# Where a block's token sums and low parts are made, GpSimd or VectorE, in a fused attention and two-layer network kernel

## The chip, the cores and the metric

The kernel runs on one core of a Trainium2 chip. The metric is the device time of one execution in microseconds. Before the change three runs took 752.82, 753.55 and 754.12 us, a median of 753.55.

## The reference, cut to what matters

Attention over 4 x 576 tokens with 8 heads of 64 gives x of 2304 tokens x 512. A first network layer follows, and a second one, which is the stage that the change touches. All is f32.

```
x = maximum(maximum(x @ w1, x @ w2), x @ w3) @ w_out        # 512 -> 768 -> 512
h = x @ w_in                                                # 512 -> 2048
g = maximum(h, 0) + alpha * minimum(h, 0)
out = g @ w_out2                                            # 2048 -> 512
```

## The kernel before, in words

f32 products are made of fp32r parts: a factor is split into a high part (a cast to fp32r) and a low part (the rest, by a subtraction), and three products (high-high, high-low, low-high) are added up in PSUM.

**The second layer** takes 2304 tokens in 3 blocks of 768 (`blk`), and 2048 hidden rows as 8 pairs of 128 rows (`q`), so there are 24 steps, n = 8 blk + q; n is counted from 0 and `NQ` is 8. Both matrix products are done by a scheme of seven products in place of eight for a 2x2 block split (`PRODUCTS`). It needs sums of quarter blocks of x: of the rows b11, b12, b21, b22 that `load_x2` fetches (four DMAs of 192 KB, 128x384 each, in this order) `sum_x2` makes four subtractions, the first of them t3 = b22 - b12, and seven tiles come of it; two halves (`half` 0 and 1) of the 512 columns are done so. `split_x2` makes high and low part of each tile. For blocks 1 and 2 the fourteen tiles go to DRAM (`xd`, L857) and come back through `fetch_x2` (L863) while the last pair of the block before is computed.

**Inside one n**, `h_products` (L1162) makes seven products, each of six matmuls of 384 columns into one PSUM bank (L1176). Two banks (tag `ph`) take turns, so a product needs the bank of the one two before it, and VectorE's addition (L1182) or ScalarE's copy (L1186) empties it. The activation (L1124 to L1128), the sums for the second matrix product (L1160) and its splits (L976 high on ScalarE, L977 low on VectorE) are queued between the products by `defer` and `due`. Behind each product the main loop (L1239) also advances `o_units`, the second matrix product of the n before, by one or two units of three matmuls of 256 columns (L983).

**At a block's end** (q = 7) `o_units` has 84 units instead of 12: the "kept" products k = 0, 1, 2 over all eight pairs (`kept_units`), whose g parts `prepare` splits a few units ahead, and the output additions (`quarter`, L1001 to L1035) with the stores (L1006). `ended` runs 48 of them ahead of the first product of n = 8, 16 and (after the last n) at the end; the other 36 follow behind the products of n = 8, five behind each. A wide kept step is a matmul of 512 columns (L989) and one of 256 (L993); a narrow one has three of 256 columns (L983). With a wide step the bank holds two halves, and each output quarter takes two additions.

**Queues.** Every engine runs its instructions in the order of the code. SyncE issues all DMAs in that order too: the weights of the first product (`load_h`, L871), of the second (`load_ow`, L883, one behind every sixth unit), output stores, and the stores and loads of the tiles. The tiles of the third block's preparation come from small pools: two row pairs (`xsp`), three sums (`tsp`) and two tiles for high and low part (`xst`).

**The third block's preparation before** goes by the table `early`: at the first product of n = 1 and n = 9 the four loads are issued; one subtraction on GpSimd (L828) stands behind each product from the fourth on; in n = 2 to 7 and 10 to 14 the first product is followed by one or two splits (L208 high on ScalarE, L211 low on GpSimd), and behind the fourth product `early_store` issues their stores. The same helpers prepare the second block earlier, in the first layer's last part, on GpSimd too.

Of the kernel before, what the change touches and what calls it, by code (L numbers as in the profile page):

```python
# [10 lines left out]
F32 = mybir.dt.float32  # L11
F32R = mybir.dt.float32r
U32 = mybir.dt.uint32
AF = mybir.ActivationFunctionType
ALU = mybir.AluOpType
# [6 lines left out]
P = 128  # L22
# [10 lines left out]
HB = BLK // 2  # L33
NBLK = NT // BLK
NQ = NF2 // 2
# [125 lines left out]
def attention_maxout_prelu_kernel(  # L161
# [13 lines left out]
    nc = tc.nc  # L175
# [41 lines left out]
    def pool(stack, name, bufs, side="left"):  # L217
        return stack.enter_context(tc.tile_pool(name=name, bufs=bufs, side=side, reuse_waits="tile"))
# [5 lines left out]
    xd = [None] + [[[dram.tile([P, 2, HB], F32, name=f"xd{blk}_{k}_{i}") for i in range(2)]  # L224
                    for k in range(7)] for blk in range(1, NBLK)]
# [455 lines left out]
    def last_net(b):  # L681
# [121 lines left out]
        for hf in range(2):  # L803
            for dc in range(NCC):
# [5 lines left out]
    PRODUCTS = (((0, 0), "11"), ((2, 256), "T2"), ((0, 256), "21"), ((2, 0), "T3"),  # L810
                ((1, 0), "T1"), ((1, 256), "T4"), ((3, 0), "22"))
    xs, x2h = {}, {}

    def load_x2(blk, i, pool, tag):

        rows = [pool.tile([P, 2, HB], F32, tag=tag, name=tag) for _ in range(2)]
        for r, t in enumerate(rows):
            for h in range(2):
                nc.sync.dma_start(t[:, h, :], x2d[2 * blk + h][:, i + 2 * r, :])
        return rows  # L820

    def sum_x2(blk, i, rows, engine, later=None):

        b11, b12, b21, b22 = (t[:, h] for t in rows for h in range(2))
        t2, t3, t4 = (tsp.tile([P, HB], F32, tag="t", name="t") for _ in range(3))
        for out_, x, y in ((t3, b22, b12), (b12, b12, b11), (t2, b22, b12), (t4, b21, t2)):
            def one(out_=out_, x=x, y=y):
                engine.tensor_tensor(out=out_, in0=x, in1=y, op=ALU.subtract)  # L828

            if later is None:  # L830
                one()
            else:
                later.append(one)
        for name, x in (("11", b11), ("T1", b12), ("21", b21), ("22", b22), ("T2", t2),
                        ("T3", t3), ("T4", t4)):
            xs[blk, name, i] = x

    def split_x2(blk, k, i, pool, tag, lo_engine=nc.vector):

        t = pool.tile([P, 2, HB], F32R, tag=tag, name=tag)  # L840
        split(t[:, 0], t[:, 1], xs.pop((blk, PRODUCTS[k][1], i)), nc.scalar, lo_engine)
        return t

    early_rows, early_parts = {}, []

    def early_load(blk, i, pool, tag):
        early_rows[blk, i] = load_x2(blk, i, pool, tag)

    def early_sums(blk, i, later=None):
        sum_x2(blk, i, early_rows.pop((blk, i)), nc.gpsimd, later)  # L850

    def early_split(blk, i, k, pool=None):
        early_parts.append((blk, k, i, split_x2(blk, k, i, pool or xst, "xst", nc.gpsimd)))

    def early_store():
        for blk, k, i, t in early_parts:
            nc.sync.dma_start(xd[blk][k][i], t.bitcast(F32))  # L857
        early_parts.clear()
# [19 lines left out]
    def load_ow():  # L878
        key = next(ow_next, None)
        if key is not None:  # L880
            _, which, a, i = key
            t = words[key] = wp.tile([P, 2, DM], F32R, tag="w", name="w")
            nc.sync.dma_start(t.bitcast(F32), (od1 if which == "o1" else od2)[a][i])  # L883
# [4 lines left out]
    for b in range(B):  # L888
        first, last = (-32, -8) if b == 0 else ((b - 1) * NUNITS + (16 if b == 1 else 3), b * NUNITS - 3)
        step = (last - first) / (len(ATT_UNITS) + 2)  # L890
# [22 lines left out]
    xsp = pool(ctx, "xsp", 2, "right")  # L913
    tsp = pool(ctx, "tsp", 3, "right")
    xst = pool(ctx, "xst", 2, "right")
# [64 lines left out]
    def o_products(g, w, off, t, bank, half, first, last):  # L980

        for i, (gi, wi) in enumerate(PAIRS):
            nc.tensor.matmul(bank[:, NH * half:NH * (half + 1)], g[:, gi, t * P:(t + 1) * P],  # L983
                             w[:, wi, off:off + NH], start=first and i == 0, stop=last and i == 2)
# [54 lines left out]
    def o_units(n):  # L1039
        blk, q = divmod(n, NQ)  # L1040
        if q == NQ - 1:

            first = [ps_h.tile([P, DM], F32, tag="ph", name="ph") for _ in range(2)]
            for p in range(2):
                yield from kept_units(blk, 0, p, first, parts_.pop((blk, 0, p)))
        for k in range(4):
            w = words[blk, "o1", q, k // 2]
            for t in range(3):
                s = 3 * k + t
                if q == 0 and s % 2 == 0:  # L1050
                    accs[s // 2] = ps_o.tile([P, DM], F32, tag="po", name="po")
                o_products(gts[n, k], w, NH * (k % 2), t, accs[s // 2], s % 2,
                           q == 0 and s % 2 == 0, q == NQ - 1 and s % 2 == 1)
                if q == NQ - 1 and s % 2 == 1:
                    for z in (s - 1, s):
                        drains.append((blk, *divmod(z, 3), accs[s // 2], z % 2))
                if k % 2 == 1 and t == 2:
                    load_ow()
                yield
            if q == NQ - 1 and k > 0:  # L1060
                prepare(blk)
        if q < NQ - 1:
            return
        for k in range(3):
            wide = [None, [0, 1, 2], [0, 1] if blk == NBLK - 1 else [0, 1, 2]][k]
            banks = [ps_o.tile([P, DM], F32, tag="po", name="po") for _ in range(3)] if k else first
            for p in range(0 if k else 2, NQ):
                for _ in range(1 if k == 0 or p == 0 else 2):
                    if len(parts_) < AHEAD:
                        prepare(blk)  # L1070
                yield from kept_units(blk, k, p, banks, parts_.pop((blk, k, p)), wide)
# [3 lines left out]
    def kept_units(blk, k, p, banks, g, wide=None):  # L1075
        w = words[blk, "o2", k, p // 2]
        for t in range(3):
            if wide is None:
                o_products(g, w, NH * (p % 2), t, banks[t // 2], t % 2,
                           p == 0 and t % 2 == 0, p == NQ - 1 and t > 0)  # L1080
            elif t in wide:
                wide_products(g, w, NH * (p % 2), t, banks[t], p == 0, p == NQ - 1)
            else:
                o_products(g, w, NH * (p % 2), t, banks[t], 0, p == 0, p == NQ - 1)
            if p == NQ - 1 and wide is not None:
                drains.append((blk, 4 + k, t, banks[t], None if t in wide else 0))
            elif p == NQ - 1 and t > 0:
                for z in ((0, 1) if t == 1 else (2,)):
                    drains.append((blk, 4 + k, z, banks[z // 2], z % 2))
            if p % 2 == 1 and t == 2:  # L1090
                load_ow()
            last = k == 2 and p == NQ - 1
            if t == 2 or last:
                for _ in drains[:] if last else drains[:2]:
                    quarter(*drains.pop(0))
            yield
# [131 lines left out]
    def ended(outs):  # L1228
        for i in range(48):
            if i in (0, 2, 4, 6, 8):  # L1230
# [1 line left out]
                due(i == 8)  # L1232
            next(outs, None)

    early = {1: [(0, None)], 2: [(0, 0)], 3: [(0, 1)], 4: [(0, 2)], 5: [(0, 3), (0, 4)], 6: [(0, 5)], 7: [(0, 6)],
             9: [(1, None)], 10: [(1, 0)], 11: [(1, 1), (1, 2)], 12: [(1, 3)], 13: [(1, 4), (1, 5)], 14: [(1, 6)]}
    sums_left = []
    outs = iter(())
    for n in range(NQ * NBLK):  # L1239
        blk, q = divmod(n, NQ)  # L1240
        units_before = [i * 12 // 7 for i in range(8)]
        if blk and q == 0:
            ended(outs)
            units_before = [5 * i + (i == 7) for i in range(8)]
        for i, _ in enumerate(h_products(n)):
            if q == NQ - 1 and blk + 1 < NBLK:
                fetch_x2(blk + 1, i)
            if i == 0:
                for half, k in early.get(n, ()):
                    if k is None:  # L1250
                        early_load(2, half, xsp, "xs")
                        early_sums(2, half, sums_left)
                    else:
                        early_split(2, half, k)
            if i == 3:
                early_store()
            if i > 2 and sums_left:
                sums_left.pop(0)()
            for _ in range(units_before[i + 1] - units_before[i]):
                next(outs, None)  # L1260
        assert next(outs, None) is None
        outs = o_units(n)
# [55 lines left out]
```

## Time and profile before

| what | before |
|---|---|
| median of 3 runs | 753.55 us (752.82 to 754.12) |
| the profiled execution's own time | 751.83 us |
| its span, first to last instruction | 750.0 us |
| TensorE (PE) busy | 733.9 us, 98% |
| VectorE (DVE) busy | 641.4 us, 86% |
| ScalarE (ACT) busy | 461.8 us, 62% |
| GpSimd (POOL) busy | 53.1 us, 7% |
| granted TensorE clock, mean | 1.000 |

PE is the matmuls, PEld the weight loads beside them, SPq the DMA issues of SyncE. Times in rows are microseconds from the span's start, the duration of one instruction is in microseconds or, in lists of one line's instructions, in ns. The bracket at a row's end is the idle time of the engine before it and what ended it. The end of a matmul is modelled, so the pace of TensorE is read from start to start. The second layer begins at 387.7 us.

### The profile page before, as it was taken

To read this page: it belongs to the slowest core of one execution; us is meant where nothing else is said; L and a number is where in the kernel's file an instruction comes from. 1 tells how busy PE (TensorE), PEld (TensorE's weight loads), DVE (VectorE), ACT (ScalarE), POOL (GpSimd) and SP (SyncE) were. 2 spreads that over 40 slices of the span, in tenths; PEclk is the share of its full clock that TensorE was granted. 3 is DMA by queue.
4 is the path that set the end of the run, shared out by engine and by line. 5 is a ranking of instruction groups with operands and counts; after the bars stand their busy time and mean duration, and the time that the engine had idled before them with its cause. 6 is when DMAs were issued, how large, how long until landed. Compare 5 with 4: busy or idle time off the path is not lost.

```text
span 750.0 us, 15973 instructions
## 1 busy us (share of the span) xinstructions
PE 733.9 (98%) x5544; PEld 709.6 (95%) x5544; DVE 641.4 (86%) x1689; ACT 461.8 (62%) x1249; POOL 53.1 (7%) x64
## 2 busy tenths in 40 slices
PE   5899999999999999999999999999999999999997
PEld 4699999999999999999999999999999999999996
DVE  5899999898899899658779888888988888988897
ACT  6987889568675787332255666624665654556571
POOL 1000000000000000024504010000401000000000
PEclk9999999999999999999999999999999999999999
DMA  7576769896999865679899889999888999767362
GB/s 250 168 228 225 244 204 344 330 343 222 326 337 335 303 225 192 225 288 325 296 324 378 270 281 317 393 387 356 308 306 292 368 402 354 283 232 258 118 200 67
DMA packets 88928, 211.95 MB, mean 283 GB/s; under 512 B 11024, under 2 KB 41232, under 8 KB 88848
## 3 DMA queue, kind: packets, MB, share of 16 engines
q1 hardware_dynamic: 88848, 210.94, 80.0%
q8 instruction: 44, 0.72, 0.4%
q14 instruction: 36, 0.29, 0.1%
HBM read 154.80 MB, written 56.10 MB: 281 GB/s over the span
## 4 chain that ended last, share of the span: by engine, by line
PE 81%; DVE 7%; DMA 5%; ACT 4%; issue 2%; SPq 0%; DVEq 0%; ACTq 0%
PE ph L1176 21%; PE bank L577 19%; PE po L983 13%; PE bank L599 9%; PE bank L750 4%; PE ph L983 3%; PE po L989 3%; DMA wh<-w 3%; PE bank L314 2%; PE bank L389 2%; ACT e L329 2%; PE bank L364 2%; PE po L993 2%; DMA raw<-in_w 1%; DVE g L977 1%
## 5 line engine op out<-in xcount | busy, mean ns | idle before, releaser
L1176 PE MATMUL ph<-x,w 128*128 128x384 f32 x990 | 200.5, 337 | 1.0 <-DVE c L1182 1.0
L577 PE MATMUL bank<-x,w 128*128 128x288 f32 x1440 | 197.9, 296 | 0.2
L577 PEld LDWEIGHTS bank<-x,w 128*128 128x128 f32 x1440 | 191.9, 188 | 2.5 <-DVE w L256 0.6
L1176 PEld LDWEIGHTS ph<-x,w 128*128 128x128 f32 x990 | 166.3, 188 | 2.5 <-DVE c L1182 1.4
L983 PE MATMUL po<-w,g 128*128 128x256 f32 x888 | 130.9, 281 | 0.0
L983 PEld LDWEIGHTS po<-w,g 128*128 128x128 f32 x888 | 125.3, 189 | 0.7
L1182 DVE TENSOR_TENSOR c<-ph,c 128x384 f32<-128x384 f32 x165 | 89.1, 552 | 29.4 <-PE ph L1176 25.7
L976 ACT CAST g<-c 128x384 fp32r<-128x384 f32 x93 | 47.0, 505 | 97.0 <-DVE c L1160 53.9
L599 PE MATMUL bank<-h,w 128*128 128x288 f32 x576 | 79.3, 297 | 0.3 <-DVE nm L322 0.3
L599 PEld LDWEIGHTS bank<-h,w 128*128 128x128 f32 x576 | 76.9, 188 | 1.2 <-DVE nm L322 0.5
L253 ACT CAST w<-word 128x512 fp32r<-128x512 f32 x100 | 57.7, 590 | 26.6 <-DMA wh<-w 10.2
L329 ACT ACTIVATE e<-e,nm 96x128 f32<-96x128 f32 (+2 forms) x176 | 68.5, 403 | 8.4 <-DVE nm L322 8.4
L256 DVE TENSOR_TENSOR w<-word,w 128x512 fp32r<-128x512 f32 x100 | 62.9, 640 | 9.0 <-ACT w L253 8.8
L1124 ACT ACTIVATE c<-c 128x384 f32<-128x384 f32 x96 | 50.5, 526 | 29.1 <-DVE c L1182 28.0
L1128 DVE SCALAR_TENSOR_TENSOR c<-c 128x384 f32<-128x384 f32 x96 | 56.5, 588 | 9.2 <-ACT c L1125 9.2
L1125 ACT ACTIVATE c<-c,nalpha 128x384 f32<-128x384 f32 x96 | 59.2, 617 | 3.2
L977 DVE TENSOR_TENSOR g<-c,g 128x384 fp32r<-128x384 f32 x96 | 56.0, 583 | 0.5 <-ACT g L976 0.5
L989 PE MATMUL po<-w,g 128*128 128x512 f32 x136 | 48.8, 397 | 0.0
L448 ACT ACTIVATE word<-raw 128x512 f32<-128x512 f32 x56 | 37.7, 682 | 17.2 <-DMA raw<-in_w 13.9
L977 DVE TENSOR_TENSOR g<-k,g 128x384 fp32r<-128x384 f32 x72 | 36.9, 549 | 7.5 <-ACT g L976 7.5
L454 DVE SCALAR_TENSOR_TENSOR word<-raw,word 128x512 uint32<-128x512 uint32 x56 | 38.8, 693 | 1.9
L1160 DVE TENSOR_TENSOR k<-c 128x384 f32<-128x384 f32 x72 | 40.1, 581 | 0.0
(103 smaller groups left out, 964.4 us busy)
## 6 DMA issues: line engine op xcount, KB each, us to landing
w<-wh SPq DMA_DIRECT2D x72, 512.0 KB, 5.4
raw<-in_w SPq DMA_DIRECT2D x50, 512.0 KB, 4.8
w<-wo SPq DMA_DIRECT2D x48, 512.0 KB, 5.9
w<-wp SPq DMA_DIRECT2D x36, 512.0 KB, 6.7
wh<-w SPq DMA_DIRECT2D x24, 512.0 KB, 5.3
xd<-xst SPq DMA_DIRECT2D x28, 384.0 KB, 5.9
x<-xd SPq DMA_DIRECT2D x28, 384.0 KB, 8.0
ws<-w SPq DMA_DIRECT2D x12, 512.0 KB, 4.0
```

What stands on the lines that cost most here:

```text
L253: (nc.scalar.copy if e == "ACT" else nc.vector.tensor_copy)(out_, in_)
L256: nc.vector.tensor_tensor(out=out_, in0=x, in1=y, op=ALU.subtract)
L329: nc.scalar.activation(tl[ek][:nq, j, i, :nk], tl[ek][:nq, j, i, :nk], AF.Exp, bias=tl["nm", u][:nq, j, i:i + 1], scale=-1.0, accum_out=tl ...
L577: nc.tensor.matmul(acc, words["gate", f, g][:, wi, cc * P:(cc + 1) * P], xt[b, cc, hf][:, xi, :], start=n == 0, stop=n == 3 * NCC - 1)
L599: nc.tensor.matmul(acc, words["mix", f][:, wi, dc * P:(dc + 1) * P], st["h", hf, f][:, xi, :], start=n == 0, stop=n == 3 * NF1 - 1)
L977: return g, lambda: nc.vector.tensor_tensor(out=g[:, 1], in0=x, in1=g[:, 0].bitcast(F32), op=ALU.subtract)
L983: nc.tensor.matmul(bank[:, NH * half:NH * (half + 1)], g[:, gi, t * P:(t + 1) * P], w[:, wi, off:off + NH], start=first and i == 0, stop=l ...
L989: nc.tensor.matmul(bank.rearrange("p (s n) -> p s n", n=NH), g[:, 0, t * P:(t + 1) * P], w[:, :, off:off + NH], start=first, stop=last)
L1125: nc.scalar.activation(a, a, AF.Copy, scale=nalpha[:, f:f + 1])
L1128: nc.vector.scalar_tensor_tensor(out=a, in0=h, scalar=0.0, in1=a, op0=ALU.max, op1=ALU.add)
L1176: nc.tensor.matmul(bank, words["h", n, i][:, wi, off + c * P:off + (c + 1) * P], x2h[blk, k, c][:, xi, :], start=m == 0, stop=m == 5)
L1182: nc.vector.tensor_tensor(out=out_, in0=bank, in1=other, op=ALU.add)
```

## The change

The table `early` goes. A table `prep` says which step stands behind which product (n, i), with i counted from 0. The loads stand at (1, 0) and (8, 0). The four subtractions, now on VectorE, stand at (2, 6), (3, 1), (3, 6), (4, 1) for the first half, and at (8, 2) twice, (8, 4) and (8, 5) for the second. The high parts stay on ScalarE; the low parts go to VectorE, each followed by its own store. The first half's low parts stand at (4, 6), (5, 1), (5, 6), (6, 1), (6, 6), (7, 1), (7, 6), the second half's at (8, 6), (10, 6), (11, 1), (11, 6), (12, 1), (12, 6), (13, 1). The high part belonging to a low part at (n, 6) stands at (n, 2), that of one at (n, 1) at (n - 1, 4). Apart from that, the third block's last kept product has no wide steps any more.

```
-            wide = [None, [0, 1, 2], [0, 1] if blk == NBLK - 1 else [0, 1, 2]][k]
+            wide = [None, [0, 1, 2], [] if blk == NBLK - 1 else [0, 1, 2]][k]
...
-    early = {1: [(0, None)], 2: [(0, 0)], 3: [(0, 1)], 4: [(0, 2)], 5: [(0, 3), (0, 4)], 6: [(0, 5)], 7: [(0, 6)],
-             9: [(1, None)], 10: [(1, 0)], 11: [(1, 1), (1, 2)], 12: [(1, 3)], 13: [(1, 4), (1, 5)], 14: [(1, 6)]}
-    sums_left = []
+    prep = {}
+
+    def at(n, i, step):
+        prep.setdefault((n, i), []).append(step)
+
+    def low_part(half, k):
+        t, x = high_parts.pop((half, k))
+        nc.vector.tensor_tensor(out=t[:, 1], in0=x, in1=t[:, 0].bitcast(F32), op=ALU.subtract)
+        nc.sync.dma_start(xd[2][k][half], t.bitcast(F32))
+
+    def high_part(half, k):
+        t, x = high_parts[half, k] = (xst.tile([P, 2, HB], F32R, tag="xst", name="xst"),
+                                      xs.pop((2, PRODUCTS[k][1], half)))
+        nc.scalar.copy(t[:, 0], x)
+
+    high_parts, sums_left = {}, []
+    for half, n in ((0, 1), (1, NQ)):
+        at(n, 0, lambda half=half: early_load(2, half, xsp, "xs"))
+        at(n, 1, lambda half=half: sum_x2(2, half, early_rows.pop((2, half)), nc.vector, sums_left))
+    for n, i in ((2, 6), (3, 1), (3, 6), (4, 1), (NQ, 2), (NQ, 2), (NQ, 4), (NQ, 5)):
+        at(n, i, lambda: sums_left.pop(0)())
+    lows = ([(n, i) for n in range(4, NQ) for i in (1, 6)][1:],
+            [(NQ, 6)] + [(n, i) for n in range(NQ + 2, 2 * NQ) for i in (1, 6)][1:])
+    for half in range(2):
+        for k, (n, i) in enumerate(lows[half][:7]):
+            at(n - (i == 1), 4 if i == 1 else 2, lambda half=half, k=k: high_part(half, k))
+            at(n, i, lambda half=half, k=k: low_part(half, k))
...
         for i, _ in enumerate(h_products(n)):
             if q == NQ - 1 and blk + 1 < NBLK:
                 fetch_x2(blk + 1, i)
-            if i == 0:
-                for half, k in early.get(n, ()):
-                    if k is None:
-                        early_load(2, half, xsp, "xs")
-                        early_sums(2, half, sums_left)
-                    else:
-                        early_split(2, half, k)
-            if i == 3:
-                early_store()
-            if i > 2 and sums_left:
-                sums_left.pop(0)()
+            for step in prep.get((n, i), ()):
+                step()
             for _ in range(units_before[i + 1] - units_before[i]):
                 next(outs, None)
```

## Rows read from the trace of the kernel before

**Rows 1.** The page's first part: busy time, share of the span, instructions

```profile
PE 733.9 (98%) x5544; PEld 709.6 (95%) x5544; DVE 641.4 (86%) x1689; ACT 461.8 (62%) x1249; POOL 53.1 (7%) x64
```

**Rows 2.** Timeline of PE, products of n = 2, 3 and 10: start, duration, instruction

```profile
410.00 1.22 PE L1176 MATMUL ph<-x,w 128*128 128x384 f32 x6
...
412.55 1.33 PE L1176 MATMUL ph<-x,w 128*128 128x384 f32 x6 [0.64 <-DVE c L1182]
...
415.94 1.22 PE L1176 MATMUL ph<-x,w 128*128 128x384 f32 x6
...
422.62 1.22 PE L1176 MATMUL ph<-x,w 128*128 128x384 f32 x6
...
427.53 1.21 PE L1176 MATMUL ph<-x,w 128*128 128x384 f32 x6
...
529.71 1.22 PE L1176 MATMUL ph<-x,w 128*128 128x384 f32 x6
...
532.03 1.33 PE L1176 MATMUL ph<-x,w 128*128 128x384 f32 x6 [0.40 <-DVE c L1182]
...
535.42 1.22 PE L1176 MATMUL ph<-x,w 128*128 128x384 f32 x6
```

**Rows 3.** Timeline of POOL and DVE around n = 2

```profile
405.41 1.25 POOL L828 TENSOR_TENSOR t<-xs 128x384 f32<-128x384 f32 x1 [7.16 <-DMA xs<-x]
...
410.67 1.36 DVE L977 TENSOR_TENSOR g<-c,g 128x384 fp32r<-128x384 f32 x1
...
415.34 0.55 DVE L977 TENSOR_TENSOR g<-c,g 128x384 fp32r<-128x384 f32 x1
```

**Rows 4.** Windows: length, busy PE, PEld, DVE, ACT, POOL; PE clock, DMA share, GB/s

```profile
425.90:437.50 11.60, 11.60 (x80) 11.60 (x79) 9.66 (x20) 7.10 (x14) 1.02 (x1) 1.00 0.84 286
...
477.50:494.80 17.30, 17.30 (x134) 16.63 (x133) 16.33 (x41) 9.90 (x24) 0.00 (x0) 1.00 1.03 402
```

**Rows 5.** SyncE's timeline; then landings: L883 at 501.7, L819 at 519, L857 all

```profile
501.71 1.38 SPq L883 DMA_DIRECT2D w<-wo  x3
...
DMA to landing us min/median/max: 5.5/5.5/5.5
...
L819 SPq DMA_DIRECT2D xs<-x x4: 422/431/478, 519.3 to 520.7; - x4
...
DMA to landing us min/median/max: 4.0/4.1/4.1
...
DMA to landing us min/median/max: 4.7/6.1/9.4
```

**Rows 6.** Timeline of DVE and PE in n = 8

```profile
501.64 0.56 DVE L1182 TENSOR_TENSOR c<-ph,c 128x384 f32<-128x384 f32 x1 [1.31 <-PE ph L1176]
502.11 0.87 DVE L1001 TENSOR_TENSOR c<-po,c 128x256 f32<-128x256 f32 x2
...
507.32 0.55 DVE L1182 TENSOR_TENSOR c<-ph,c 128x384 f32<-128x384 f32 x1
...
508.79 1.21 PE L1176 MATMUL ph<-x,w 128*128 128x384 f32 x6
```

**Rows 7.** Timeline of the kernel's end

```profile
745.01 0.28 PE L993 MATMUL po<-w,g 128*128 128x256 f32 x1
...
745.21 2.00 DVE L1001 TENSOR_TENSOR m<-po,m 128x256 f32<-128x256 f32 x5 [1.89 <-PE po L989]
745.36 0.51 PE L983 MATMUL po<-w,g 128*128 128x256 f32 x3
```

**Rows 8.** Window of the last 0.2 us, as rows 4; timeline of PE at the start

```profile
749.80:750.00 0.20, 0.00 (x0) 0.00 (x0) 0.00 (x0) 0.00 (x0) 0.00 (x0) 0.50 0.00 0
...
11.18 1.30 PE L364 MATMUL bank<-ident,e 108*108 108x108 f32 x6 [2.21 <-DVE e L353]
...
14.58 1.35 PE L389 MATMUL bank<-pt,v 108*64 108x108 f32 x12
...
21.06 0.78 PE L389 MATMUL bank<-pt,v 108*64 108x108 f32 x12
```

More of the change, by code (lines that the diff above doesn't have):

```diff
@@ L847, in early_load, with early_sums @@
         early_rows[blk, i] = load_x2(blk, i, pool, tag)
-    def early_sums(blk, i, later=None):
-        sum_x2(blk, i, early_rows.pop((blk, i)), nc.gpsimd, later)
+    def early_sums(blk, i):
+        sum_x2(blk, i, early_rows.pop((blk, i)), nc.gpsimd)
     def early_split(blk, i, k, pool=None):
```

## The prediction

> **What bounds the kernel now.** I read the shares of busy time first: TensorE is busy 98% of the span [rows 1], so the rest need only keep out of its way. In the stage that the change touches (n = 0 to 23, eight n to a block) the start times of the matmul groups then show what a full pace is: the third to the sixth product of n = 3 start 4.91 us apart, 422.62 to 427.53 [rows 2]. Only twice in that whole stage does TensorE idle by more than 0.15 us, both times until a VectorE addition ends: at 412.55 (n = 2) and at 532.03 (n = 10). The same three steps took 5.94 and 5.71 us there, so the two places cost 1.03 and 0.80 us [rows 2].
>
> VectorE's timeline shows why. While GpSimd does the third block's four subtractions from 405.41 on, VectorE's additions with both inputs in SBUF take 1.36 us where they take 0.55 us else [rows 3]; VectorE falls behind, and TensorE waits for its PSUM bank. In the steady n VectorE is busy 9.66 us of 11.60, ending idle for 1.9 us [rows 4].
>
> The other thing to see is the SyncE queue around n = 8. From 477.5 to 494.8 the DMA engines are full (share 1.03) [rows 4], and the queue runs late. Its order is the code's: the last `load_ow` ahead of the first product of n = 8 (k = 1, p = 3 of the old block) is the first of the three issues at 501.71, the next two belong behind the first product [rows 5]. Yet at 501.64 VectorE already adds up the third product of n = 8 [rows 6]. So there the queue is two products behind the engines.
>
> **The change, part by part.** The profiled execution took 751.83 us (span 750.04 and what lies around it), 1.72 below the median of 753.55. The sum is made against 751.83.
>
> *GpSimd's work goes.* No third-block work is left on GpSimd, so both stalls go: −1.03 −0.80 = −1.83. Bounds: 0 if VectorE's own extra work stalled TensorE as much in the same places; not below −1.83, since TensorE shows no other idle time there.
>
> *VectorE gets 22 operations* (eight subtractions for sums, fourteen low parts) of 0.55 us [rows 3], 0.47 from one start to the next in an unbroken row (501.64 to 502.11) [rows 6]. Apart from n = 8 each n gets at most two, 0.94 us into 1.9 us of idle time [rows 4]: 0, and at most 0.5 us in all if the gaps lie badly.
>
> *ScalarE's fourteen casts* move from the start of an n to behind the third and fifth product. They were there before; only their place changes. Each takes one of two `xst` tiles, and now waits until a store has landed whose low part stands three products earlier: 4.9 us [rows 2], and some 0.6 for the rest of the way. Such stores took 4.7 to 9.4 us, median 6.1 [rows 5]. ScalarE is busy 7.10 of 11.60 us [rows 4], so a wait of 0.6 is hidden: 0, with an upper end of 1.0 us. The SyncE queue is passed by the stores: each now stands in front of weight loads that are due a whole n later, and waits for one low part at most. Price 0.
>
> *The last kept product of 256 columns.* A wide step (a matmul of 512 columns and one of 256) starts at 745.01, the next step at 745.36: 0.35 us. Three of 256 columns take 0.51, of which the first alone is 0.28, so 0.12 each and 0.35 a step: no cost on TensorE [rows 7]. Five final additions run in 2.00 us from 745.21, two each for t = 0 and 1; after the change there is one for each t. The last one may start when the last matmul is done, at 745.87 instead of 746.8, and ends by 746.3 instead of 747.21. The last store follows it: −0.9 (bounds −0.5 and −1.0).
>
> *The loads and sums at n = 8.* This is the large term. The second half's four token loads move from the first step of n = 9 to the first step of n = 8, and its first two subtractions to the third step of n = 8. In the queue the loads come right behind the first of the issues at 501.71. At 0.46 us an issue the last starts no sooner than 503.6; such a load alone took 4.0 to 4.1 us, so it can't land before 507.6 [rows 5]. The queue lands in order: the issue in front lands at 501.71 + 5.5 = 507.2 [rows 5], and the four loads, 0.5 us apart in the profile (issues 519.3 to 520.7, landings 4.0 to 4.1 later), end at 509.2. Two more stores of low parts (384 KB, 1.0 us each by the same pace) now fall into the full stretch; as the stretch ahead of it isn't quite full, I count 1.2 of these 2.0. So the last load lands at R = 510.4 (507.6 to 511.2).
>
> The page on DMA: Bandwidth & Descriptors of the Trainium skill (Anatomy of one DMA, on those that GpSimd issues) gives some 2 us fixed and 436 GB/s; for 192 KB that would be an estimate of 2.5 us and R = 506.1, a stall 4.3 us shorter than below. The loads in this profile took 4.0 at the least, and the row decides.
>
> The first subtraction needs the fourth load (b22). VectorE reaches it at 502.11, right behind the addition of 501.64, and waits. Behind it on VectorE stand twelve output additions and the addition that empties the bank of the fourth product; from 502.11 to its start at 507.32 VectorE works without a pause, 5.21 us [rows 6]. With the two subtractions (0.94) and that addition (0.54) the bank is free at R + 6.7 = 517.1. The sixth product needs this bank and started at 508.79 [rows 6]. So TensorE starts it 8.3 us late (5.5 to 9.1), and since TensorE is the bound from there on, all of it stays.
>
> *TensorE's clock.* After the last matmul (745.36 + 0.51) [rows 7] TensorE idles, and at 749.8 the granted clock is 0.50, which is 1.2 GHz [rows 8]. The stall idles it for longer than these 3.9 us, as the products' units run out of low parts that VectorE holds up too. At the start of the kernel twelve matmuls of 108x108 took 1.35 us at 14.58 and 0.78 later [rows 8], with TensorE at work from 11.18 on; so up to about 4.7 us at half pace, a loss of 2.3. Lower end 0. I take 2.0, since the stall is far longer than the idle time before the fall.
>
> The page TensorE: Matmul & The Clock Gate of the Trainium skill (What's actually happening) calls half rate the default that activity lifts. The end of this trace agrees; no run here shows it inside a kernel.
>
> *The other sums of n = 8 and its low part*, 3 x 0.47 = 1.4 us behind the fifth, sixth and seventh product, meet a VectorE that is just late: between 0 and 1.4, I take 0.4, as its waits for ScalarE (2 us in that n) are then over.
>
> Sum: 751.83 − 1.83 − 0.9 + 8.3 + 2.0 + 0.4 = 759.8. With 1.72 more, **761.5 us**.
>
> **The rivals.** *No wait at n = 8.* If the four loads land before VectorE gets there, only the gains are left: 751.83 − 1.83 − 0.9 + 0.4 = 749.5, or 751.2 as a median, faster. This decides at about R = 504.5, where the stall eats the gains. For it speaks that two products lie between the load and the sums in the code, and a load that is issued in time lands in 4.1 us [rows 5]; against it that the issue in front of them is at 501.71 in the trace. Chance 0.10.
>
> *ScalarE waits for the xst tiles.* If the stores land in 7.4 us rather than 6.1, a cast waits 1.9 us, and 1.1 of it passes on to the addition that TensorE waits for; with six such places 6.6 us, and no stall at n = 8: 749.5 + 6.6 = 756.1, or 757.8. For it speaks the 9.4 in the rows, against it that stores outside the full stretch mostly took about 6. Chance 0.05.
>
> *A short wait*, R near 504.5 by a queue that catches up in part: no change, 753.5. Chance 0.03. That the change doesn't do what it says can't weigh: GpSimd's calls are gone from the loop, though at n = 8 the sums stand behind the third, fifth and sixth product.
>
> **How the numbers follow.** A measurement of this kernel can tell some 0.2%, 1.5 us, from no change. The forecast has 0.82. Its ends: stall 5.5, clock 0, nothing else: 754.6 + 1.7 = 756.3; stall 9.1, clock 2.3, 1.4 in n = 8 and 1.5 for ScalarE and VectorE: 763.4 + 1.7 = 765.1. Range 756.0 to 765.0, which takes in the second rival. Faster 0.11, within 0.2% 0.04, slower 0.85.
>
> **What would show it.** Right: in the profile after, no GpSimd work past 400 us, TensorE at full pace through n = 2 and 10; at n = 8 a VectorE subtraction at line 828 behind a wait of about 8 us for the token load, the sixth product of n = 8 about 8 us late, and a granted clock of 0.5 for some microseconds there; three final additions. Wrong: token loads issued well before 500, or a sum that starts at its place without idle time in front; then the first rival holds.

## The result, and the profile after

The changed kernel takes 761.54 us (median of 6 runs, 760.71 to 764.98), the kernel before 753.27 us (6 runs): a ratio of 1.0114, with a 95% interval of 1.0090 to 1.0138. It is slower by 8.3 us.

The profiled execution of the changed kernel is the longest of its six, 764.98 us with a span of 763.3. Its second layer starts at 392.19 us, 4.5 us later than before, though no code ahead of it changed. So traces are compared below by **the stage**: from the first product of n = 0 to the end of the span. It took 362.35 us before and 371.09 us after, +8.74 us.

The first part of the page after (busy time, share of the span, instructions) and its line of granted clock:

```profile
PE 738.7 (97%) x5560; PEld 714.1 (94%) x5560; DVE 639.2 (84%) x1709; ACT 462.5 (61%) x1249; POOL 28.0 (4%) x42
...
PEclk9999999999999999999999999997999999999999
```

GpSimd's 22 operations and 25.1 us are gone [rows 1]. VectorE has 20 instructions more and is busy 2.2 us less. One slice of the clock line, two thirds into the span, is below 9. TensorE's waits of over 0.15 us in the whole stage, by what ended them (us in total, times, longest):

```profile
PE po L993 <- DVE g L977: 6.1, 1, 6.1
PE ph L1176 <- DVE c L1182: 1.0, 1, 1.0
PE po L993 <- DMA w<-wp: 0.5, 1, 0.5
```

The two waits of before (n = 2 and n = 10) are not among these. Timeline of PE after, the third to the sixth product of n = 2, and of n = 10:

```profile
414.89 1.22 PE L1176 MATMUL ph<-x,w 128*128 128x384 f32 x6
...
419.80 1.21 PE L1176 MATMUL ph<-x,w 128*128 128x384 f32 x6
...
544.37 1.22 PE L1176 MATMUL ph<-x,w 128*128 128x384 f32 x6
...
549.28 1.21 PE L1176 MATMUL ph<-x,w 128*128 128x384 f32 x6
```

Both take 4.91 us, the full pace of n = 3 [rows 2]. The three waits above are all in n = 8. Timeline of PE there; the rows of line 1176 are its first, second, fifth, sixth and seventh product and the first of n = 9 (the second product's row is cut at the window's edge):

```profile
498.63 1.21 PE L1176 MATMUL ph<-x,w 128*128 128x384 f32 x6
...
500.31 0.35 PE L993 MATMUL po<-w,g 128*128 128x256 f32 x1 [0.47 <-DMA w<-wp]
...
502.15 0.34 PE L1176 MATMUL ph<-x,w 128*128 128x384 f32 x1
...
510.55 1.21 PE L1176 MATMUL ph<-x,w 128*128 128x384 f32 x6
...
519.27 0.58 PE L993 MATMUL po<-w,g 128*128 128x256 f32 x1 [6.10 <-DVE g L977]
...
521.31 2.29 PE L1176 MATMUL ph<-x,w 128*128 128x384 f32 x6 [1.04 <-DVE c L1182]
...
526.46 1.21 PE L1176 MATMUL ph<-x,w 128*128 128x384 f32 x6
...
529.62 1.21 PE L1176 MATMUL ph<-x,w 128*128 128x384 f32 x6
```

A step from one product to the next took 2.80 us before; the fifth product, for one, with the sixth at 508.79 [rows 6] (timeline of PE before):

```profile
505.99 1.21 PE L1176 MATMUL ph<-x,w 128*128 128x384 f32 x6
```

Now the fifth to the sixth takes 10.76, which is 7.96 more; the sixth to the seventh 5.15 (+2.35); the first to the second 3.52 (+0.72). Counted from the start of n = 8 the sixth product comes after 22.68 us instead of 14.00, so it is 8.68 us late: 0.72 of that lie in the first step and 7.96 in the fifth. VectorE's timeline shows what the fifth and the sixth step hang on:

```profile
506.19 0.56 DVE L1182 TENSOR_TENSOR c<-ph,c 128x384 f32<-128x384 f32 x1 [1.31 <-PE ph L1176]
514.44 0.56 DVE L828 TENSOR_TENSOR t<-xs 128x384 f32<-128x384 f32 x1 [7.68 <-DMA xs<-x]
515.03 0.56 DVE L828 TENSOR_TENSOR xs<-xs 128x384 f32<-128x384 f32 x1
...
518.66 0.55 DVE L977 TENSOR_TENSOR g<-k,g 128x384 fp32r<-128x384 f32 x1
...
520.71 0.55 DVE L1182 TENSOR_TENSOR c<-ph,c 128x384 f32<-128x384 f32 x1
```

The first subtraction of the sums stands idle 7.68 us for the token loads. The low part that TensorE wants next (518.66) and the addition that frees the sixth product's bank (520.71) are queued behind it. The loads themselves, from SyncE's timeline, and behind it line 819's DMAs in that stretch (who waited for them, in us and times; us from issue to landing):

```profile
507.03 0.38 SPq L883 DMA_DIRECT2D w<-wo  x1
507.46 2.12 SPq L819 DMA_DIRECT2D xs<-x  x4
```

```profile
  DVE t L828: 7.7, 1
  ACT xst L1248: 4.9, 1
...
DMA to landing us min/median/max: 5.1/5.3/5.4
```

They are issued at 507.5 to 509.2, 9 to 11 us after n = 8 has begun, though the code has them behind its first product. SyncE itself waited for 8.1 of the 15 us from 497 to 512 until DMAs issued earlier had landed, 5.3 of them for the kept product's weights. ScalarE waited 4.9 us for them as well, with the cast that now stands at (8, 2). The clock, by windows (columns as in [rows 4]):

```profile
516.10:526.20 10.10, 5.90 (x18) 5.00 (x19) 8.64 (x21) 2.88 (x6) 0.00 (x0) 0.50 0.58 204
526.50:529.60 3.10, 3.10 (x19) 2.85 (x18) 3.10 (x7) 2.57 (x6) 0.00 (x0) 1.00 0.83 280
```

It is at 0.50, which is 1.2 GHz, for the 10.1 us up to the seventh product, and back at 1.00 behind it. The end of the kernel after, three final additions and three stores:

```profile
759.12 1.14 DVE L1001 TENSOR_TENSOR m<-po,m 128x256 f32<-128x256 f32 x3 [1.92 <-PE po L983]
...
759.57 1.30 SPq L1006 DMA_DIRECT2D out_dram<-m  x3
```

TensorE's last matmul ends at 759.80, 3.5 us ahead of the span's end; before it was 4.16 us.

### The profile page after: what moved, and what is told of

It is laid out like the page before. It is cut to its first block, busy times and chain, and to the rows that moved or that the text cites. A ratio compares the mean times of both kernels' runs of the same rounds, so it can differ in the third digit from the quotient of the medians.

```text
span 763.3 us, 15977 instructions
## 1 busy us (share of the span) xinstructions
PE 738.7 (97%) x5560; PEld 714.1 (94%) x5560; DVE 639.2 (84%) x1709; ACT 462.5 (61%) x1249; POOL 28.0 (4%) x42
## 4 chain that ended last, share of the span: by engine, by line
PE 80%; DVE 7%; DMA 6%; ACT 5%; issue 1%; SPq 0%; DVEq 0%; ACTq 0%
PE ph L1176 21%; PE bank L577 21%; PE po L983 14%; PE bank L599 7%; PE ph L983 3%; PE bank L750 3%; PE po L989 3%; ACT e L329 2%; PE bank L314 2%; PE bank L389 2%; PE bank L364 2%; PE po L993 1%; DMA wh<-w 1%; DVE t L730 1%; DMA w<-wp 1%
## 5 line engine op out<-in xcount | busy, mean ns | idle before, releaser
L983 PE MATMUL po<-w,g 128*128 128x256 f32 x936 | 135.5, 281 | 0.0
L983 PEld LDWEIGHTS po<-w,g 128*128 128x128 f32 x936 | 130.1, 189 | 0.3
L599 PE MATMUL bank<-h,w 128*128 128x288 f32 x576 | 81.0, 300 | 0.5 <-DVE nm L322 0.5
L1128 DVE SCALAR_TENSOR_TENSOR c<-c 128x384 f32<-128x384 f32 x96 | 53.2, 554 | 6.5 <-ACT c L1125 6.5
L977 DVE TENSOR_TENSOR g<-c,g 128x384 fp32r<-128x384 f32 x96 | 52.9, 551 | 0.5 <-ACT g L976 0.5
L989 PE MATMUL po<-w,g 128*128 128x512 f32 x120 | 44.4, 408 | 0.0
L993 PE MATMUL po<-w,g 128*128 128x256 f32 x120 | 34.2, 289 | 6.6 <-DVE g L977 6.1
```

The costliest lines, as they stand in the source:

```text
L599: nc.tensor.matmul(acc, words["mix", f][:, wi, dc * P:(dc + 1) * P], st["h", hf, f][:, xi, :], start=n == 0, stop=n == 3 * NF1 - 1)
L977: return g, lambda: nc.vector.tensor_tensor(out=g[:, 1], in0=x, in1=g[:, 0].bitcast(F32), op=ALU.subtract)
L989: nc.tensor.matmul(bank.rearrange("p (s n) -> p s n", n=NH), g[:, 0, t * P:(t + 1) * P], w[:, :, off:off + NH], start=first, stop=last)
L1128: nc.vector.scalar_tensor_tensor(out=a, in0=h, scalar=0.0, in1=a, op0=ALU.max, op1=ALU.add)
```

## The experiments

The theory (T1): the second half's loads land too late for the place of the sums; VectorE, which works in order, waits, and that is the loss. Rivals: VectorE's 22 added operations cost by themselves; the fallen clock is a large part; ScalarE's casts are what holds the rest. Edits are against the changed kernel unless said otherwise. All results (the kernel before measured 752.69 to 753.52 us beside them; stage as above, by one profile each):

| run | median us | ratio to before (95%) | stage us |
|---|---|---|---|
| e1: second half one n later | 751.83 | 0.9986 (0.9968 to 1.0003) | 361.70 |
| e2: narrow last product alone | 752.21 | 0.9985 (0.9974 to 0.9995) | 362.19 |
| e3: load earlier | 757.99 | 1.0055 (1.0031 to 1.0079) | 367.84 |
| e4: sums behind the landing | 758.01 | 1.0070 (1.0051 to 1.0088) | 366.21 |
| e5: filler in the wait | 761.40 | 1.0110 (1.0087 to 1.0132) | 370.71 |
| e6: first half's change alone | 754.02 | 1.0018 (0.9995 to 1.0042) | 361.83 |
| e7: e1 on GpSimd | 751.67 | 0.9982 (0.9967 to 0.9998) | 362.62 |
| e8: e1, first half sooner | 749.86 | 0.9951 (0.9934 to 0.9968) | 360.44 |
| e9: e4 with the cast later | 753.66 | 0.9999 (0.9985 to 1.0012) | 362.25 |
| e10: cast later alone | 763.78 | 1.0127 (1.0087 to 1.0167) | 370.90 |
| e11: filler in all of the wait | 761.29 | 1.0098 (1.0062 to 1.0135) | 370.40 |
| e12: e8 on GpSimd | 751.59 | 0.9975 (0.9958 to 0.9991) | 359.79 |

One profile's stage also holds what lies far from every edit: n = 0 and 1 together take 18.86 to 19.62 us in these profiles, and n = 7 of e7 and n = 16 of e8 are 0.8 us longer than in the others. So small differences are read from single n and steps below.

**e1: the second half's steps one n later.** The loads go behind the seventh product of n = 8, the sums to n = 9 to 11, where the first half has them in n = 2 to 4.

```
-    for half, n in ((0, 1), (1, NQ)):
-        at(n, 0, lambda half=half: early_load(2, half, xsp, "xs"))
+    for half, load, n in ((0, (1, 0), 1), (1, (NQ, 6), NQ + 1)):
+        at(*load, lambda half=half: early_load(2, half, xsp, "xs"))
...
-    for n, i in ((2, 6), (3, 1), (3, 6), (4, 1), (NQ, 2), (NQ, 2), (NQ, 4), (NQ, 5)):
+    for n, i in ((2, 6), (3, 1), (3, 6), (4, 1), (NQ + 1, 6), (NQ + 2, 1), (NQ + 2, 6), (NQ + 3, 1)):
...
-            [(NQ, 6)] + [(n, i) for n in range(NQ + 2, 2 * NQ) for i in (1, 6)][1:])
+            [(n, i) for n in range(NQ + 3, 2 * NQ) for i in (1, 6)][1:])
```

> The change, with the second half of the third block moved out of n = 8: load at the last step of n = 8, sums in n = 9 to 11, low parts in n = 11 to 14. Theory 1 (at n = 8 VectorE waits for token loads that a late DMA queue issues late): no VectorE wait of over 0.5 us for xs, no stall in n = 8, clock at full, and all the gains: about 750.5 us, 2.7 below the kernel before. Theory 2 (22 more VectorE operations cost TensorE wherever they stand): 755 us or more, with many short idle times of TensorE before line 1176.

All 22 operations are still on VectorE, and the stage is 9.4 us shorter than after the change. The only wait of TensorE in it, and not one on VectorE:

```profile
PE po L993 <- DMA w<-wp: 1.2, 1, 1.2
```

So the place of the loads and sums at n = 8 is the loss, and the added operations are not. The time expected was lower, though: the wait for a kept product's weights, 0.5 us after the change, is 1.2 here and takes back most of the gain.

**e2: only the narrow last product**, in the kernel before.

```
-            wide = [None, [0, 1, 2], [0, 1] if blk == NBLK - 1 else [0, 1, 2]][k]
+            wide = [None, [0, 1, 2], [] if blk == NBLK - 1 else [0, 1, 2]][k]
```

> The kernel before, with only the last kept product made narrow. Theory: three final additions in place of five, the end 0.6 to 0.9 us earlier, about 752.6 us, near what can be told; TensorE's last steps keep 0.35 us each. Rival: the extra matmul and weight load of a narrow step costs TensorE time (16 x 0.1 us): 754 us or more.

The time from the last matmul to the end of the span falls from 4.16 to 3.41 us: −0.75.

**e3: the loads earlier**, behind the seventh product of n = 7.

```
+    at(1, 0, lambda: early_load(2, 0, xsp, "xs"))
...
-        at(n, 0, lambda half=half: early_load(2, half, xsp, "xs"))
...
+    at(NQ - 1, 6, lambda: early_load(2, 1, xsp, "xs"))
```

> The change, with the second half's four token loads issued behind the last step of n = 7, ahead of some ten other DMAs; sums and low parts stay where the change put them. Theory 1: the loads land before VectorE reaches the sums in n = 8, the wait there is under 1 us and the 7 us stall goes; the four loads push the kept product's weights back by about 2 us, of which TensorE may feel 0 to 2: 750.5 to 753 us. Theory 2 (it is the sums' and casts' own place in n = 8 that costs, not the queue's lateness): 759 to 761 us.

The time lies between the two that were expected. VectorE now finds its data: the subtraction starts without idle time, and the step from the fifth to the sixth product is down from 10.76 to 2.99 us. But TensorE waits for something else, at the first units of n = 8 (timelines of PE and DVE, then a window):

```profile
499.71 0.55 PE L993 MATMUL po<-w,g 128*128 128x256 f32 x1 [2.88 <-DMA w<-wp]
...
508.79 0.55 DVE L828 TENSOR_TENSOR t<-xs 128x384 f32<-128x384 f32 x1
```

```profile
498.90:505.70 6.80, 5.99 (x19) 5.44 (x20) 0.49 (x2) 0.08 (x1) 0.00 (x0) 0.50 1.03 406
```

The loads sit in the full DMA stretch (share 1.03) in front of the weights, and those come 2.88 us late; the clock falls too. T1's mechanism holds, but its way out does not: room for 768 KB must be taken from something there.

**e4: the loads as in the change, the sums two products later.**

```
-    for n, i in ((2, 6), (3, 1), (3, 6), (4, 1), (NQ, 2), (NQ, 2), (NQ, 4), (NQ, 5)):
+    for n, i in ((2, 6), (3, 1), (3, 6), (4, 1), (NQ, 4), (NQ, 4), (NQ, 5), (NQ, 5)):
```

> The change, with the two subtractions behind the third product of n = 8 moved behind the fifth (two there, two behind the sixth); load and ScalarE's first cast stay. Theory 1: the loads land about when VectorE gets there, its wait is under 1.5 us; ScalarE's cast still waits for the first load and holds the next cast of a kept part, so TensorE idles up to 2 us in n = 8: 751 to 753.5 us. Rival (the wait moves along with the sums): 757 us or more. If ScalarE's wait costs nothing: 750.5 us.

The time is the rival's (757 us or more), but not for the rival's reason: VectorE no longer waits for the loads at all. The timelines of ScalarE and VectorE name a second holder, and the two longest of PE's waits show the price:

```profile
512.59 0.51 ACT L1248 CAST xst<-xs 128x384 fp32r<-128x384 f32 x1 [4.90 <-DMA xs<-x]
...
513.55 0.56 DVE L977 TENSOR_TENSOR g<-k,g 128x384 fp32r<-128x384 f32 x1 [3.90 <-ACT g L976]
```

```profile
PE ph L1176 <- DVE c L1182: 1.4, 1, 1.4
PE po L993 <- DVE g L977: 1.3, 1, 1.3
```

ScalarE's first cast of the second half stands at (8, 2) and waits for the same loads. Behind it stands the high part without which VectorE can't make the low part that TensorE needs.

**e9: e4, with that cast moved to (8, 4) as well. e10: the cast alone moved, the sums as in the change.**

```
-            at(n - (i == 1), 4 if i == 1 else 2, lambda half=half, k=k: high_part(half, k))
+            at(n - (i == 1), 4 if i == 1 or n == NQ else 2, lambda half=half, k=k: high_part(half, k))
```

> As e4_sums_after_landing, with ScalarE's first cast of the second half also moved, from behind the third to behind the fifth product of n = 8. Theory (in e4 VectorE's 3.9 us wait was for ScalarE, which stood behind that cast's wait for the first token load): no VectorE wait of over 1 us, no clock fall, the short wait for weights stays: 750.5 to 752 us. Rival (the wait moves along again): 756 us or more.

> The change, with ScalarE's first cast of the second half alone moved from behind the third to behind the fifth product of n = 8; the subtractions stay behind the third. Theory (VectorE's own wait for the loads is enough): TensorE as late as in the change, 760.5 to 762 us. Rival (ScalarE's cast is what holds the low parts that TensorE needs): 758 us or less.

With both moved the stage is 8.8 us shorter than after the change, and no long wait is left in n = 8. The time, 753.66 us, is still above what was expected: n = 9 takes 13.33 us for 11.79 before, as late sums now meet it (timeline of PE):

```profile
522.23 1.31 PE L1176 MATMUL ph<-x,w 128*128 128x384 f32 x6 [1.16 <-DVE c L1182]
```

With the cast alone moved nothing is gained: TensorE still waits 6.08 us for VectorE, and the time, 763.78 us, is above the range expected (four runs, 760.72 to 765.72). So either of the two engines is enough to hold TensorE, VectorE for the longer time.

**e5 and e11: the clock.** TensorE multiplies by a matrix of zeros while it would wait, and adds that to a bank that is open, in e5 with 48 matmuls in one place, in e11 with 52 and 12 in both places of the wait. The core of e11:

```
+    nc.vector.tensor_tensor(out=ident_r, in0=ident, in1=ident, op=ALU.subtract)
...
+                if (blk, k, p) == (0, 2, 4):
+                    fill.append((banks[0][:, :NH], words[blk, "o2", k, 2][:, 0, :NH]))
+                    filler(52)
...
+            nc.tensor.matmul(fill[0][0], ident_r, fill[0][1], start=False, stop=False)
...
+            if (n, i) == (NQ, 4):
+                filler(12)
```

> The change, with 48 matmuls of zero weights (256 columns, added to a bank that is being summed up, so they add nothing) ahead of the unit at which TensorE begins its long wait in n = 8; they take 5.6 us of the 6.1 us wait. Theory (the fallen clock is a cost of its own, some 2.5 us on top of the wait): the granted clock stays at 1.00 in n = 8 or falls for less time, and the kernel is 1.5 to 2.5 us faster than the change, 759 to 760 us. Rival (the clock costs nothing, since VectorE sets the pace after the wait): 761.5 us, no difference.

> As e5_filler, with 52 matmuls of zero weights in the first wait of n = 8 and 12 more in the second one, ahead of the sixth product, so that TensorE hardly idles. Theory (a fallen clock costs 2.4 us in the change, and only idle TensorE makes it fall): granted clock 1.00 throughout n = 8, from the sixth to the seventh product 2.8 us instead of 5.15, and 759 to 760 us. Rival (what follows the wait is paced by VectorE): the clock stays up, 5 us from the sixth to the seventh product all the same, 761.5 us.

In e5 the clock still fell, behind waits of 0.61 and 1.42 us that the filler left. In e11 it did not (timeline of PE: fillers, sixth and seventh product; then windows):

```profile
508.73 6.06 PE L1113 MATMUL po<-w,ident_r 128*128 128x256 f32 x52
...
515.43 1.57 PE L1113 MATMUL po<-w,ident_r 128*128 128x256 f32 x12
517.02 1.31 PE L1186 MATMUL ph<-x,w 128*128 128x384 f32 x6
...
520.49 1.31 PE L1186 MATMUL ph<-x,w 128*128 128x384 f32 x6
...
529.28 1.32 PE L1186 MATMUL ph<-x,w 128*128 128x384 f32 x6 [0.44 <-DVE c L1192]
```

```profile
517.00:523.70 6.70, 6.54 (x34) 5.53 (x35) 5.41 (x12) 3.87 (x8) 0.00 (x0) 1.00 0.97 327
523.70:536.20 12.50, 12.06 (x80) 11.74 (x80) 12.11 (x28) 6.78 (x15) 0.00 (x0) 1.00 1.00 355
```

The sixth to the seventh product takes 3.47 us instead of 5.15. But from the seventh on TensorE runs into a VectorE that is late: n = 9 takes 12.42 us (523.76 to 536.18) instead of 11.59. From the sixth product to n = 10 it is 19.16 us at full clock, 19.90 after the change and 17.76 before. So 0.7 us hangs on the clock in the end, and 1.4 us is lost without it. e5 and e10, with the same long wait, lie between: 19.19 us with some 3.4 us at a clock of 0.50, and 19.57 with 6.8, where the change has some 10. In the times no gain shows: the ratio to before is 1.0098 in e11 and 1.0114 for the change, and their intervals overlap.

**e6: the first half's change alone**, in the kernel before (sums and low parts of half 0 on VectorE at the places of the change; the second half on GpSimd as before).

> The kernel before, with the first half alone prepared as in the change (VectorE, one at a time); the second half stays on GpSimd from n = 9 and the last product wide. Theory: the stall of n = 2 goes (1.0 us), that of n = 10 stays, and the three stores in n = 6 and 7 make TensorE wait 0.5 to 1.2 us for weights in n = 8: between 752.5 and 753.8 us, no difference that can be told. Rival (the first half's change is a clear gain): 752 us or less.

The time, 754.02 us, is 0.2 above the range and can't be told from that of before. The stall of n = 2 is gone, and the waits left in the stage are these:

```profile
PE po L993 <- DMA w<-wp: 0.7, 1, 0.7
PE ph L1176 <- DVE c L1182: 0.2, 1, 0.2
```

So the wait for weights at n = 8 comes with the first half's new places, not with the second half.

**e8: e1 with the first half's sums and low parts sooner**, the low parts from (3, 1) to (6, 1).

```
-    for n, i in ((2, 6), (3, 1), (3, 6), (4, 1), (NQ, 2), (NQ, 2), (NQ, 4), (NQ, 5)):
+    for n, i in ((2, 1), (2, 1), (2, 6), (2, 6), (NQ + 1, 6), (NQ + 2, 1), (NQ + 2, 6), (NQ + 3, 1)):
...
-    lows = ([(n, i) for n in range(4, NQ) for i in (1, 6)][1:],
+    lows = ([(n, i) for n in range(3, NQ) for i in (1, 6)],
```

> As e1_half_one_later, with the first half's sums in n = 2 and its low parts from n = 3 to 6, so that none of its stores falls into the full DMA stretch of n = 7. Theory (the stores there push the kept product's weights back, for which TensorE waited 1.2 us in e1): no wait for w<-wp in n = 8, and 1.0 to 1.5 us less than e1, some 750.5 us, 2.5 below the kernel before. Rival (the wait for weights comes from elsewhere): as e1, 751.8 us.

This is faster than both kernels; than the one before by 0.5%. The first half's seven stores, after the change and then in e8 (first and last start):

```profile
L1243 SPq DMA_DIRECT2D xd<-xst x7: 319/320/326, 448.0 to 491.1; - x7
```

```profile
L1243 SPq DMA_DIRECT2D xd<-xst x7: 319/320/320, 426.4 to 460.9; - x7
```

After the change the last ones fall into the full stretch ahead of n = 8 (DMA share 1.03 from 477.5 to 498.6); before, the last was issued at 474.8, some 20 us ahead of it. In e8 the weights of n = 8 are in time, n = 8 takes 19.97 us where e1 took 21.45, and n = 2 and n = 10 run at full pace. This profile has a wait of 0.57 us for such weights at n = 16, where e1, with the same steps there, has none.

**e7 and e12: the places of e1 and of e8, with sums and low parts on GpSimd.**

```
-        nc.vector.tensor_tensor(out=t[:, 1], in0=x, in1=t[:, 0].bitcast(F32), op=ALU.subtract)
+        nc.gpsimd.tensor_tensor(out=t[:, 1], in0=x, in1=t[:, 0].bitcast(F32), op=ALU.subtract)
...
-        at(n, 1, lambda half=half: sum_x2(2, half, early_rows.pop((2, half)), nc.vector, sums_left))
+        at(n, 1, lambda half=half: sum_x2(2, half, early_rows.pop((2, half)), nc.gpsimd, sums_left))
```

> The schedule of e1_half_one_later (one step at a time, second half out of n = 8, narrow last product), with the sums and low parts on GpSimd as before. Theory (GpSimd slows VectorE's additions from 0.55 to 1.36 us, and four in a row were too much for VectorE's idle time): one at a time each costs VectorE 0.8 us of 1.9 us idle time, so at most short waits in n = 2 and 10, and the time is within 0.5 us of e1's. Then the gain is in the spreading, not in the engine. Rival (any GpSimd operation beside VectorE stalls TensorE): 0.2 us or more at each of 22, 755 us or more.

> The schedule of e8_first_half_sooner (no third-block work in n = 8, first half's stores ahead of the full DMA stretch, narrow last product) with sums and low parts on GpSimd as before. Theory (the places of loads, stores and casts decide, the engine hardly): four GpSimd sums still run in a row once their loads have landed, which costs TensorE some 0.2 to 0.5 us at n = 2 and 10 as in e7, no waits else: 750 to 751.5 us, at most 1 us above e8. Rival (VectorE in GpSimd's place is what made e8 fast): 752.5 us or more.

e7 did not spread GpSimd's work as meant. Its timeline of POOL (first and last sum) shows them in one row as soon as the loads have landed, since GpSimd has nothing else to hold it:

```profile
407.44 1.16 POOL L828 TENSOR_TENSOR t<-xs 128x384 f32<-128x384 f32 x1 [7.26 <-DMA xs<-x]
...
411.06 1.21 POOL L828 TENSOR_TENSOR t<-xs,t 128x384 f32<-128x384 f32 x1
```

n = 2 still takes 11.81 us there, for 12.62 before. e12 has no wait of TensorE over 0.12 us in the stage. Its time is 1.7 us above e8's, where at most 1 was expected; the intervals of the two ratios overlap, and its stage is the shorter one. e7 and e1 measure the same (751.67 and 751.83 us). So the places of loads, casts and stores decide; that the engine makes no difference at all is not shown, but it is small beside the 11.0 us by which n = 8 grew.

## Why the prediction was right

- **GpSimd's stalls, −1.83.** n = 2 is 1.04 us and n = 10 0.80 us shorter. The term held. (GpSimd still makes three casts for n = 0, the last at 402.44.)
- **VectorE's 22 operations, 0.** Held: no wait in the steady n, and e1 with all 22 of them is no slower than the kernel before.
- **ScalarE's casts, 0.** No price was paid, but one step was missing: the cast at (8, 2) was only costed for its `xst` tile, while it waited 4.90 us for its data. The wait of VectorE beside it hid that (e10); with that one gone it shows (e4). The rival that ScalarE waits for `xst` tiles did not come about: ScalarE has no such wait of over 0.15 us in the stage after. The fourteen stores took 2.6 to 7.8 us to land, with a median of 3.0, where 6.1 was counted.
- **The last product, −0.9.** Inside its bounds, but too large: −0.68 in the changed kernel and −0.75 in e2. The last addition ends 0.46 us behind the last matmul instead of 1.34, so 0.88 was right for it; three store issues in a row from 759.57 then take SyncE until 760.87, and the last starts at 760.5, not with the addition's end at 760.26. The narrow steps were not quite free: n = 23 takes 0.07 us more, which leaves −0.61.
- **The loads at n = 8, +8.3.** Measured +8.68, counted from the start of n = 8, which is 3.84 us later than before in this execution. So the landing at 514.4 is R = 510.6 (predicted 510.4), and the bank is free 6.8 us behind it (predicted 6.7). The steps inside R came out too: the DMA in front, issued at 507.03, landed 5.3 us later, which is 508.5 when the 3.84 are taken off (predicted 507.2 + 1.2), and the last load 2.1 us behind it (predicted 2.0). All 553 DMAs land in the order of their issue in both traces. Each load took 5.1 to 5.4 us from issue to landing, where 4.0 to 4.1 stood for one alone.
  The Trainium skill's page DMA: Bandwidth & Descriptors (Anatomy of one DMA) would have had 2.5 us for such a load, an estimate from its fit for DMAs that GpSimd issues; in a SyncE queue with others in flight it took twice that, and the measurement decides.
- **The clock, +2.0.** The sixth to the seventh product took 2.35 us more, with the clock at 0.50 for 10.1 us. This step was right in place and size, but e11 shows that it doesn't add up with the next one: without the fall 1.4 of the 2.1 us that are lost behind the sixth product (19.90 against 17.76 us) stay, as VectorE is late.
  The Trainium skill's page TensorE: Matmul & The Clock Gate (What's actually happening) has half rate as the default that activity lifts; the windows of n = 8 now show it inside the kernel, 0.50 from inside the wait up to the seventh product and 1.00 behind it.
- **Other work in n = 8, +0.4.** Mis-sized as a term: late VectorE alone costs 1.4 (e11). With the clock, 2.1 for the forecast's 2.4. The reason given for the small size, that VectorE's waits for ScalarE would be over, held only in small part: they were 1.77 us before (1.05 and 0.72) and are 1.28 after (1.04 and 0.24), since ScalarE was held up by VectorE in its turn (timelines of ACT and DVE after):

```profile
521.81 0.51 ACT L976 CAST g<-c 128x384 fp32r<-128x384 f32 x1 [8.03 <-DVE c L1128]
...
522.77 1.03 DVE L977 TENSOR_TENSOR g<-k,g 128x384 fp32r<-128x384 f32 x2 [1.04 <-ACT g L976]
```

- **What was missing:** the wait for the kept product's weights, +0.72 in the step from the first to the second product. The prediction counted the two stores that move into the full stretch as a delay for the token loads (1.2 us), not for the weights that stand in the same queue. e6 has this wait with the first half's change alone, and e8 has none in n = 8. After the change the 8.68 us hold it already; weights and loads are late together. In e5, e10 and e11 the first step takes 3.84 to 4.36 us and the fifth 10.71 to 10.75 all the same, so no run shows what in-time weights alone would have saved there.

The stage moved by +8.74 us for +7.97 by the sum. The terms make up half of the difference: +0.38 at the loads, +0.29 at the last product, −0.26 behind the sixth product. The other half, +0.41, lies in n = 0 and 1, ahead of every step that was moved, and the profiles differ by as much there with the same code. So the mechanism and its largest terms were right; that the forecast of 761.5 us meets a median of 761.54 is luck, with runs from 760.71 to 764.98 us and errors of both signs in the sum. The rival of no wait at n = 8 fell by the 7.68 us in front of the subtraction.

## What to carry to other kernels

Read from the trace when a queue really issues a load, not how many products lie between load and use in the code: here it did so two to three products late, and one early use on an engine that works in order held up everything queued there. Look for every consumer of that load on every engine, since behind the first holder a second may stand (ScalarE's cast, worth 3.9 us on VectorE). A preparation that runs ahead should have its stores out before a stretch where the DMA engines are full; moving it sooner was worth 1.5 us of n = 8 (e1 to e8), while which of the two engines made it is not clearly seen in the times.

## What the runs showed that was not expected

**More work, less busy time.** VectorE has 22 operations more and two additions less, yet is busy 639.2 us after and 641.4 before. While GpSimd works, VectorE's own operations are stretched [rows 3]; after the change that is over (line 977 in the stage, shortest, median and longest in ns), and in e12, with GpSimd's operations at e8's places, it is back:

```profile
L977 DVE TENSOR_TENSOR g<-c,g x96: 544/551/560, 399.5 to 734.5; 128x384 fp32r<-128x384 f32 x96
```

```profile
L977 DVE TENSOR_TENSOR g<-c,g x96: 542/550/1376, 394.6 to 719.0; 128x384 fp32r<-128x384 f32 x96
```

e12's VectorE is busy 640.4 us without the 22 operations, e8's 639.5 us with them: on VectorE they cost nothing in sum. That buys little, since TensorE had felt it in two places only (1.83 us), and hardly feels it in e12, where n = 2 takes 11.73 us for 11.58.

**The clock fell after short waits.** In e4 two waits of 1.26 and 1.43 us, ended at 514.16 and 516.21, have the clock at 0.50 from 515.16 on; in e1 one wait of 1.24 us left it at 1.00. A fall need not cost what the slower matmuls take: in n = 8 its net price was 0.7 us, for 10.1 us at half the clock, as VectorE was late there in any case.
